# Attention with talking heads and two MLPs: loads of v halved and doubled in number, scatters and weight stores regrouped

## The chip, the cores and the metric

The program runs on one core of one Trainium2 chip. The metric is the time of one execution on the device, in microseconds; the median of 3 runs stands for a kernel. One execution was also taken by the hardware profiler, and all rows below are of that one. The engines are named as the profile names them: PE (TensorE, with its weight loads as PEld), DVE (VectorE), ACT (ScalarE), POOL (GpSimd) and SP (SyncE), whose queue issues nearly all DMAs here.

## What is computed

Four batches, twelve heads, 448 rows, 64 values a head. Scores of all heads are mixed by a 12x12 matrix before the softmax and its result by another one after it; then come the product with v and two MLPs over 1792 tokens of 768 values.

```python
scores = scale * np.matmul(q, k.transpose(0, 1, 3, 2))
scores = np.einsum('bhij,hg->bgij', scores, w_pre)
scores = scores - np.max(scores, axis=-1, keepdims=True)
attn = np.exp(scores)
attn = attn / (np.sum(attn, axis=-1, keepdims=True) + 1e-09)
attn = np.einsum('bhij,hg->bgij', attn, w_post)
out = np.matmul(attn, v)
# x: out as (tokens, heads * values)
x = (1 / (1 + np.exp(-(x @ w_gate))) * (x @ w_val)) @ w_out
h = np.maximum(x @ w_in, 0.0)
y = h * h @ w_out2
```

All is in float32; where PE multiplies in a faster format (fp32r), an operand is split into a rounded part and its remainder (gh and gl, wh and wl, xh and xl) and three products are summed.

## The kernel before

**Tiles and groups.** A batch's 448 rows are cut into four tiles of 110, 110, 110 and 118 rows; sixteen tiles in all. For a tile, `scores` (L162) multiplies q and k for six pairs of heads; the result of each head is copied out of PSUM into a tile `e` (even heads of a pair by ACT, L176, odd ones by DVE, L174), and a DMA scatters it into `g` (L181), where a partition holds one row of one head and ten rows of all twelve heads make a *group* of 120 partitions. A tile has 11 groups, the fourth one 12, the last of only 8 rows; 180 groups in all. There are three `e` buffers, of two heads each.

**The loop.** `attention` writes its instructions in an order laid out by hand, one step s a group: `premix` (L206) of group s, `maximum` (L214) on DVE, `exponent` (L222) on ACT, `normal` (L228 to L233) on DVE and POOL, `split` of group s + 2 (cast gh on ACT, L196; remainder gl on POOL, L197), then, as a small planner of costs in microseconds allows (`STEP`, `PW`, `VW`, `SW`), the six `scores` of the next tile, `postmix` (L248) of earlier groups and `values` (L277). Two tiles are a *chunk*; when the postmix of a chunk's last group is done, six value steps of two heads each follow, one a step, and each result is stored to `xs` (L293). Chunks 0, 2, 4 and 6 are the first halves of the batches; their value steps fall where the scores of the batch's fourth tile are computed and scattered.

**Loads of v.** `v_load` (L267) brings `HV` = 4 heads in one DMA of 448 KB into one of two buffers; a chunk needs three. The two first of the program are loaded at s = 4 and 6, each further one after the value step that frees a buffer.

**Scatter of the fourth tile.** 118 rows in order r, r + 10, r + 20, ...: 8 places of a group have 12 rows and 2 have 11, so a head goes out as two DMAs, 8x12 rows and 2x11 rows. The other tiles take one, 10x11.

**Queues.** Every engine, and SP's queue with it, works in the order written. A DMA that must wait for its source, for a free buffer or for the eighth DMA before it holds up all that stand behind it on the same queue.

**The MLP beside it.** `mlp` is a generator, advanced by `whole` while attention still runs: attention yields 1 (every third step from step 68 on), 2 (each step once the last scores are done) or 3 (in the tail), and `EACH` says how many steps of the MLP a yield of each kind may take. These steps load x tiles of finished batches (L559), split them (cast xh on ACT L575, remainder xl on POOL or DVE L576) and prepare the first weights. A weight passes seven stages: load (`w_load`, L451), `w_bias` (ACT), `w_high` and `w_low` (DVE), `w_sum` (POOL, L501; the sum is also stored to `ws`, L502, for the second half of the tokens), `w_round` (ACT, L508) and `w_rest` (POOL, L514). In the MLP's own stage a `tick` before each product advances the even stages and the odd ones in turn.

Of the kernel before, what the change touches and what calls it, by code (L numbers as in the profile page):

```python
# [7 lines left out]
F32 = mybir.dt.float32  # L8
# [8 lines left out]
P = 128  # L17
JP = 112
GI = 10
HV = 4  # L20
LAG = 3
LA = 5
NA = 9
# [1 line left out]
KB = 10  # L25
EARLY = 112
EM = 2
EACH = (1, 2, 2)


def row_tiles(S):
# [3 lines left out]
    return list(zip(cuts, cuts[1:]))  # L35


def row_order(i0, i1):

    return [i for r in range(GI) for i in range(i0 + r, i1, GI)]  # L40


def attention(tc, q, k, v, w_pre, w_post, xs, B, H, S, D):
# [10 lines left out]
    nc = tc.nc  # L54
    JT = S // JP
# [19 lines left out]
    with ExitStack() as ctx, ExitStack() as mid, ExitStack() as left:  # L75
        kw = dict(side="right")
        one = ctx.enter_context(tc.tile_pool(name="a_one", bufs=1, **kw))
        pv = ctx.enter_context(tc.tile_pool(name="a_v", bufs=2, **kw))
        po = ctx.enter_context(tc.tile_pool(name="a_o", bufs=4, **kw))
        pp = ctx.enter_context(tc.tile_pool(name="a_p", bufs=1, **kw))  # L80
        pa = mid.enter_context(tc.tile_pool(name="a_a", bufs=NA, **kw))
# [32 lines left out]
        def mixers():  # L114
            wp32 = p0.tile([KM, GI, H], F32, name="wp32")
            nc.vector.tensor_tensor(
                out=wp32, in0=mask, in1=wr[:, 0:1, :].to_broadcast([KM, GI, H]), op=ALU.mult
            )
            nc.vector.tensor_scalar(out=wp32, in0=wp32, scalar1=SCALE, scalar2=None, op0=ALU.mult)
            x = wp32.rearrange("p i g -> p (i g)")  # L120
            nc.vector.tensor_copy(wp[0], x)
            nc.vector.tensor_tensor(out=wp[1], in0=x, in1=wp[0].bitcast(F32), op=ALU.subtract)
            nc.vector.tensor_tensor(
                out=wq.rearrange("p g i -> p i g"),
                in0=mask,
                in1=wr[:, 1:2, :].to_broadcast([KM, GI, H]),
                op=ALU.mult,
            )
# [14 lines left out]
            nc.sync.dma_start(out=q_t[n][:, p0:p1, :isz], in_=x[:, p0:p1])  # L143


        g_t = {}

        def scores(n, p):

            b, i0, isz = tiles[n]  # L150
            if p == 0:
                g_t[n] = pg.tile([KM, GT, S], F32, tag="g", name="g")
            kt = k_t.pop((b, p)) if i0 + isz == S else k_t[b, p]
            ps = [
                ps_b.tile([P, S], F32, tag="b", name="ps_s")
                if n == 0 and p % 2
                else ps_q.tile([P, S], F32, tag="q", name="ps_s")
                for _ in range(2)
            ]
            for o in range(2):  # L160
                r = slice(o * D, (o + 1) * D)
                nc.tensor.matmul(  # L162
                    ps[o][:isz], lhsT=q_t[n][r, p, :isz], rhs=kt[r], start=True, stop=True
                )
            if n == 0 and p >= 3:
                e = [pa.tile([IM, S], F32, tag="a", name="e0") for _ in range(2)]
            else:
                t = p4.tile([IM, 2, S], F32, tag="e", name="e")
                e = [t[:, o] for o in range(2)]
            ng, rest = divmod(isz, GI)  # L170
            to = g_t[n].rearrange("(r h) g j -> h r g j", h=H)
            for o in range(2):
                if o:
                    nc.vector.tensor_copy(e[o][:isz], ps[o][:isz])  # L174
                else:
                    nc.scalar.copy(e[o][:isz], ps[o][:isz])  # L176
                queue = nc.scalar if n == 0 and o and p in (1, 3, 4, 5) else nc.sync
                for r0, r1, g in ((0, rest, ng + 1), (rest, GI, ng)):
                    if r0 < r1:
                        e0 = r0 * (ng + 1)  # L180
                        queue.dma_start(  # L181
                            out=to[2 * p + o, r0:r1, :g], in_=e[o][e0 : e0 + (r1 - r0) * g]
                        )


        a_t = {}
# [76 lines left out]
        vraw = {}  # L263

        def v_load(c, hv):
            t = pv.tile([JP, HV, JT, D], F32, tag="vraw", name="vraw")
            nc.sync.dma_start(out=t, in_=v[chunks[c][0], hv])  # L267
            vraw[c, hv] = t

# [69 lines left out]
        for p in range(NP):  # L339
            scores(0, p)  # L340
        mixers()
        q_load(1)
        for s in range(2):
            split(s)
        for s in range(NG + 30):
            if s < NG:
                premix(s)
            flush()
            if s < NG:
                maximum(s)  # L350
            if s in (4, 6):
                load_next(v_load, v_order)
            if 8 <= s < 8 + KB - NP:
                load_next(k_load, k_order)
            if 1 <= s <= NG:
                exponent(s - 1)
            if 2 <= s < NG + 2:
                normal(s - 2)
            if s + 2 < NG:
                split(s + 2)  # L360
            left_over = STEP - MW
            ready = front and front[0][0] <= s
            if ready and due(s):
                next_scores()
                ready, left_over = False, left_over - SW
            fresh = None
            while bpos < len(back) and (left_over > 0.5 or s >= NG):
                f, cost, *x = back[bpos]
                if f is postmix:
                    if x[0] > s - LAG:  # L370
                        break
                    fresh = groups[x[0]][3]
                elif x[0] == fresh:
                    if s < NG:
                        break
                    flush()
                if len(pending) > 3:
                    flush()
                f(*x)
                if f is values and (x[1] + 2) % HV == 0:  # L380
                    pending.append((load_next, v_load, v_order))
                bpos += 1
                left_over -= cost
                if f is postmix and x[0] == NG - 1:
                    flush()
                    mid.close()
                if s >= NG:
                    yield 3 if bpos == len(back) or back[bpos][0] is values else 2
            if ready and left_over > 0.4:
                next_scores()  # L390
            if not front and not closed:
                left.close()
                closed = True
            if NG - EARLY <= s < NG:
                if closed:
                    yield 2
                elif s % 3 == 0:
                    yield 1
# [3 lines left out]
def mlp(tc, xs, wg, wv, wo, wi2, wo2, out, DM, DF1, DF2):  # L402
# [6 lines left out]
    nc = tc.nc  # L409
# [5 lines left out]
    with ExitStack() as ctx:  # L415
# [83 lines left out]
        def w_sum(n):  # L499
            s, x = size(n), w32[n]  # L500
            nc.gpsimd.tensor_tensor(out=x[:, s], in0=x[:, s], in1=fs.pop(n)[:, s], op=ALU.add)  # L501
            nc.sync.dma_start(out=ws[n, :, s], in_=x[:, s])  # L502

        def w_round(n):
            s = size(n)
            h = pw.tile([P, KC, P], F32R, tag="wh", name="wh")
            lo = pw.tile([P, KC, P], F32R, tag="wl", name="wl")
            nc.scalar.copy(h[:, s], w32[n][:, s])  # L508
            ready[n] = (h, lo)

        def w_rest(n):
            s = size(n)
# [288 lines left out]
```

## Time and profile before

| | |
|---|---|
| median of 3 runs | 1525.56 us (1524.79 to 1530.44) |
| the profiled execution | 1525.78 us, span 1524.1 us |
| busy: PE, DVE, ACT, POOL | 1473.3, 804.6, 580.3, 709.0 us |
| PE busy in the first 50 us | 33.3 us |
| PE busy from 50 to 500 us | 420.6 of 450 us |
| PE busy from 550 us to the end | 970.5 of 974 us |

A row of a timeline gives the start in us from the program's start, the duration, the engine and line, what is written and read, how many instructions are merged, and in brackets how long the engine was idle before it and what ended that. SPq and ACTq are the queues of SP and ACT: the row is the issue of a DMA, not its transfer. Matmuls are pipelined and their ends modelled, so rows of PE overlap a little. A wait is put down to the semaphore that came last by the profile; at a cast that waits for many scatters at once the name shown can be that of another DMA.

### The profile page before, as it was taken

Reading aid. Unit: us, or ns where it says so; the run is one execution under the profiler, and the core shown is the slowest. Engines: PE = TensorE matmul, PEld = TensorE weight load, DVE = VectorE, ACT = ScalarE, POOL = GpSimd, SP = SyncE. Lnnn points to the kernel's source line nnn. Section 1 sums busy time; section 2 is a strip of 40 time slices with the busy share of each in tenths; the row PEclk is TensorE's granted clock in tenths of the full one; section 3 lists DMA queues with packets and bytes.
Section 4 is the critical chain, followed back from the end, with each engine's and each line's share of the span. In section 5 each row is a group of like instructions: output and inputs, shape, how many; then the busy total and the mean of one; then the engine's idle time right before and its main releaser. Section 6 shows DMA issues by size and latency. Waiting matters only on the chain.

```text
span 1524.1 us, 21978 instructions
## 1 busy us (share of the span) xinstructions
PE 1473.3 (97%) x8028; PEld 1248.1 (82%) x8028; DVE 804.6 (53%) x1367; ACT 580.3 (38%) x1192; POOL 709.0 (47%) x583
## 2 busy tenths in 40 slices
PE   6989979999997999999999999999999999999999
PEld 2666747667676889999999999999999999999998
DVE  3747748667675576768889998921111101333000
ACT  3645645655654333332334443312222111333111
POOL 3756647657766455454545555532222222223221
PEclk8999989999998999999999999999999999999999
DMA  5554554555534254444444456632112111112221
GB/s 168 151 156 127 144 157 119 160 166 149 159 117 122 80 168 159 174 156 165 156 157 163 165 163 197 218 111 63 52 52 63 52 46 59 52 52 62 77 71 41
DMA packets 84400, 185.47 MB, mean 122 GB/s; under 512 B 17348, under 2 KB 54212, under 8 KB 84292
## 3 DMA queue, kind: packets, MB, share of 16 engines
q1 hardware_dynamic: 83812, 183.28, 38.3%
q8 instruction: 63, 1.03, 0.3%
q10 hardware_dynamic: 480, 0.79, 0.1%
q14 instruction: 45, 0.37, 0.1%
HBM read 107.75 MB, written 37.75 MB: 95 GB/s over the span
## 4 chain that ended last, share of the span: by engine, by line
PE 90%; DMA 5%; POOL 1%; issue 1%; DVE 1%; SPq 1%; ACT 1%; ACTq 0%; POOLq 0%
PE ps L643 66%; PE ps_p L248 8%; PE ps_m L206 6%; PE ps_s L162 5%; PE ps_v L277 4%; DMA xr<-xs 1%; DMA vraw<-in_v 1%; DMA q<-in_q 1%; DMA g<-e 1%; POOL gl L197 1%; DMA k<-in_k 1%; SPq L181 1%; POOL wn L233 1%; DVE xl L576 0%; DVE e L174 0%
## 5 line engine op out<-in xcount | busy, mean ns | idle before, releaser
L514 POOL TENSOR_TENSOR wl<-w,wh 128x768 fp32r<-128x768 f32 (+1 forms) x140 | 258.6, 1849 | 553.9 <-ACT wh L508 546.0
L643 PE MATMUL ps<-xh,wh 128*128 128x448 f32 x960 | 352.2, 367 | 0.0
L643 PE MATMUL ps<-xh,wl 128*128 128x448 f32 x960 | 351.7, 366 | 0.0
L643 PE MATMUL ps<-xl,wh 128*128 128x448 f32 x960 | 351.7, 366 | 0.0
L643 PE MATMUL ps<-hh,wl 128*128 128x448 f32 x672 | 247.0, 368 | 0.0
L643 PE MATMUL ps<-hl,wh 128*128 128x448 f32 x672 | 247.0, 368 | 0.0
L643 PE MATMUL ps<-hh,wh 128*128 128x448 f32 x672 | 246.9, 367 | 0.0
L197 POOL TENSOR_TENSOR gl<-g,gh 120x448 fp32r<-120x448 f32 x180 | 208.0, 1156 | 23.5 <-ACT gh L196 23.5
L248 PEld LDWEIGHTS ps_p<-wn,a 120*112 120x112 f32 (+1 forms) x1440 | 164.2, 178 | 39.3 <-issue 18.7
L643 PEld LDWEIGHTS ps<-xh,wh 128*128 128x128 f32 x960 | 180.4, 188 | 16.5 <-issue 1.0
L643 PEld LDWEIGHTS ps<-xh,wl 128*128 128x128 f32 x960 | 180.4, 188 | 15.4 <-POOL wl L514 0.2
L643 PEld LDWEIGHTS ps<-xl,wh 128*128 128x128 f32 x960 | 180.5, 188 | 14.9
L248 PE MATMUL ps_p<-wn,a 120*112 120x120 f32 (+1 forms) x1440 | 176.5, 271 | 2.7 <-POOL wn L233 2.7
L233 POOL TENSOR_SCALAR wn<-wq,sm 120x120 f32<-120x120 f32 x180 | 107.1, 595 | 153.2 <-DVE sm L231 114.0
L214 DVE TENSOR_REDUCE nm<-ps_m 120x1 f32<-120x448 f32 x180 | 111.9, 622 | 96.6 <-PE ps_m L206 96.4
L501 POOL TENSOR_TENSOR w<-w,w_f 128x768 f32<-128x768 f32 (+1 forms) x70 | 135.4, 1934 | 58.5 <-DVE w_f L490 58.5
L206 PE MATMUL ps_m<-gh,wp 120*120 120x448 f32 x360 | 121.4, 419 | 18.0 <-ACT gh L196 10.7
L661 DVE TENSOR_TENSOR ps<-ps,sg 128x448 f32<-128x448 f32 x48 | 30.4, 632 | 201.8 <-PE ps L643 201.8
L643 PEld LDWEIGHTS ps<-hh,wh 128*128 128x128 f32 x672 | 126.3, 188 | 11.5
L643 PEld LDWEIGHTS ps<-hl,wh 128*128 128x128 f32 x672 | 126.3, 188 | 11.5
L643 PEld LDWEIGHTS ps<-hh,wl 128*128 128x128 f32 x672 | 126.2, 188 | 11.5
L222 ACT ACTIVATE a<-ps_m,nm 120x448 f32<-120x448 f32 x180 | 114.7, 637 | 42.3 <-DVE nm L214 41.4
(45 smaller groups left out, 1690.2 us busy)
## 6 DMA issues: line engine op xcount, KB each, us to landing
g<-e SPq DMA_DIRECT2D x140, 192.5 KB
ws<-w SPq DMA_DIRECT2D x58, 384.0 KB
w<-ws SPq DMA_DIRECT2D x58, 384.0 KB
w_raw<-in_wo SPq DMA_DIRECT2D x18, 768.0 KB
w_raw<-in_wi SPq DMA_DIRECT2D x16, 768.0 KB
vraw<-in_v SPq DMA_DIRECT2D x24, 448.0 KB
w_raw<-in_wg SPq DMA_DIRECT2D x12, 768.0 KB
w_raw<-in_wv SPq DMA_DIRECT2D x12, 768.0 KB
```

Of the source, the lines that this page charges most:

```text
L162: nc.tensor.matmul(ps[o][:isz], lhsT=q_t[n][r, p, :isz], rhs=kt[r], start=True, stop=True)
L197: nc.gpsimd.tensor_tensor(out=lo[:kk], in0=x, in1=hi[:kk].bitcast(F32), op=ALU.subtract)
L206: nc.tensor.matmul(ps[:kk], lhsT=wp[w][:kk, :kk], rhs=x, start=m == 0, stop=m == 2)
L214: nc.vector.tensor_reduce(out=nm[:kk], in_=ps[:kk], op=ALU.max, axis=AX.X, negate=True)
L222: nc.scalar.activation(a[:kk], ps[:kk], AF.Exp, bias=nm[:kk], accum_out=sm[:kk])
L233: nc.gpsimd.tensor_scalar(out=wn[:kk], in0=wq[:kk], scalar1=sm[:kk], scalar2=None, op0=ALU.mult)
L248: nc.tensor.matmul(ps[:JP, jt], lhsT=a[:kk, jt * JP : (jt + 1) * JP], rhs=wn[:kk].rearrange("p g i -> p (g i)"), start=True, stop=True,)
L277: nc.tensor.matmul(ps[o * D : (o + 1) * D, :w], lhsT=vraw[c, (h + o) // HV][:, (h + o) % HV, jt, :], rhs=ap[c][:, jt, h + o, :w], start=jt ...
L501: nc.gpsimd.tensor_tensor(out=x[:, s], in0=x[:, s], in1=fs.pop(n)[:, s], op=ALU.add)
L514: nc.gpsimd.tensor_tensor(out=lo[:, s], in0=w32.pop(n)[:, s], in1=h[:, s].bitcast(F32), op=ALU.subtract)
L643: nc.tensor.matmul(ps, lhsT=a, rhs=x, start=first and n == 0, stop=last and n == total - 1)
L661: nc.vector.tensor_tensor(out=pv, in0=pv, in1=sg[c], op=ALU.mult)
```

## The change

- `HV` is 2: v comes in six loads a chunk instead of three, 224 KB each, into four buffers (as many bytes as before). The first four are issued at s = 4, 5, 6 and 7; each further one after every value step.
- Rows of a tile are ordered by whole groups: the fourth tile's head goes out as one DMA of 10x11 rows and one of its last 8 rows.
- The first tile of the program is scattered in two passes: groups 0 to 3 at once (40 rows a head), groups 4 to 10 (70 rows) after all six pairs and the mixers, and before the q load of the second tile.
- A yield of kind 2 takes one step of the MLP instead of two.
- The store of a prepared weight moves from `w_sum` to `w_round`.

```diff
-HV = 4
+HV = 2
-EACH = (1, 2, 2)
+EACH = (1, 1, 2)
...
-def row_order(i0, i1):
-
-    return [i for r in range(GI) for i in range(i0 + r, i1, GI)]
+def blocks(b, i0, i1):
+
+    n = (i1 - i0) // GI
+    return [(0, 4), (4, n)] if b == i0 == 0 else [(0, n)]
+
+
+def row_order(b, i0, i1):
+
+    rows = []
+    for g0, g1 in blocks(b, i0, i1):
+        rows += [i0 + g * GI + r for r in range(GI) for g in range(g0, g1)]
+    return rows + list(range(i0 + len(rows), i1))
...
-        pv = ctx.enter_context(tc.tile_pool(name="a_v", bufs=2, **kw))
+        pv4 = ctx.enter_context(tc.tile_pool(name="a_v", bufs=4, **kw))
...
-                queue = nc.scalar if n == 0 and o and p in (1, 3, 4, 5) else nc.sync
-                for r0, r1, g in ((0, rest, ng + 1), (rest, GI, ng)):
-                    if r0 < r1:
-                        e0 = r0 * (ng + 1)
-                        queue.dma_start(
-                            out=to[2 * p + o, r0:r1, :g], in_=e[o][e0 : e0 + (r1 - r0) * g]
-                        )
+                e0 = 0
+                for m, (g0, g1) in enumerate(blocks(b, i0, i0 + isz)):
+                    e1 = e0 + (g1 - g0) * GI
+                    move = (to[2 * p + o, :, g0:g1], e[o][e0:e1])
+                    if m:
+                        second.append(move)
+                    else:
+                        queue = nc.scalar if n == 0 and o and p in (1, 3, 4, 5) else nc.sync
+                        queue.dma_start(out=move[0], in_=move[1])
+                    e0 = e1
+                if e0 < isz:
+                    nc.sync.dma_start(out=to[2 * p + o, : isz - e0, g1], in_=e[o][e0:isz])
...
         mixers()
+        for x, y in second:
+            nc.sync.dma_start(out=x, in_=y)
         q_load(1)
...
-            if s in (4, 6):
+            if s in (4, 5, 6, 7):
                 load_next(v_load, v_order)
...
             nc.gpsimd.tensor_tensor(out=x[:, s], in0=x[:, s], in1=fs.pop(n)[:, s], op=ALU.add)
-            nc.sync.dma_start(out=ws[n, :, s], in_=x[:, s])
...
             ready[n] = (h, lo)
+            if n < once:
+                nc.sync.dma_start(out=ws[n, :, s], in_=w32[n][:, s])
```

The order on PE is the same in both kernels. On SP's queue, at the program's start, before (g is the group tile, e a score copy, wr the two mixing matrices):

```order
L101 DMA wr<-in_w_post 120x1x12
L181 DMA g<-e 10x11x448 x5
L181 DMA g<-e_183 10x11x448
L181 DMA g<-e_193 10x11x448
L181 DMA g<-e_203 10x11x448
L143 DMA q<-in_q 128x6x110
L181 DMA g<-e 10x11x448 x8
```

and now:

```order
L110 DMA wr<-in_w_post 120x1x12
L193 DMA g<-e 10x4x448 x5
L193 DMA g<-e_183 10x4x448
L193 DMA g<-e_193 10x4x448
L193 DMA g<-e_203 10x4x448
L356 DMA g<-e 10x7x448 x6
L356 DMA g<-e_183 10x7x448
L356 DMA g<-e_184 10x7x448
L356 DMA g<-e_193 10x7x448
L356 DMA g<-e_194 10x7x448
L356 DMA g<-e_203 10x7x448
L356 DMA g<-e_204 10x7x448
L152 DMA q<-in_q 128x6x110
```

The q load of the second tile has moved behind twelve more scatters. SP's queue at chunk 0's value steps, from the fifth pair of heads of the fourth tile on, before:

```order
L181 DMA g<-e 8x12x448
L181 DMA g<-e 2x11x448
L135 DMA k<-in_k 128x448
L293 DMA xs_57<-xo 128x220 x2
L267 DMA vraw<-in_v 112x1024
L181 DMA g<-e 8x12x448
L181 DMA g<-e 2x11x448
L181 DMA g<-e 8x12x448
L181 DMA g<-e 2x11x448
```

and now:

```order
L193 DMA g<-e 10x11x448
L196 DMA g<-e 8x448
L144 DMA k<-in_k 128x448
L306 DMA xs_57<-xo 128x220
L280 DMA vraw<-in_v 112x512
L306 DMA xs_57<-xo 128x220
L280 DMA vraw<-in_v 112x512
L193 DMA g<-e 10x11x448
L196 DMA g<-e 8x448
L193 DMA g<-e 10x11x448
L196 DMA g<-e 8x448
```

A half load of v now stands behind each store of a value step, the first of them one store sooner. On ACT at chunk 6's value steps, from the third value copy xo on, before:

```order
L292 COPY xo<-ps_v 128x220
L222 ACTIVATE a,sm<-ps_m,nm 120x448
L196 CAST gh<-g 120x448
L575 CAST xh<-xr 128x448
L508 CAST wh<-w_3880 128x768
L292 COPY xo<-ps_v 128x220
L222 ACTIVATE a,sm<-ps_m,nm 120x448
L196 CAST gh<-g 120x448
L575 CAST xh<-xr 128x448
```

and now, from the fourth on:

```order
L305 COPY xo<-ps_v 128x220
L235 ACTIVATE a,sm<-ps_m,nm 120x448
L209 CAST gh<-g 120x448
L591 CAST xh<-xr 128x448
L522 CAST wh<-w_3920 128x768
L305 COPY xo<-ps_v 128x220
L235 ACTIVATE a,sm<-ps_m,nm 120x448
L209 CAST gh<-g 120x448
L305 COPY xo<-ps_v 128x220
L235 ACTIVATE a,sm<-ps_m,nm 120x448
L209 CAST gh<-g 120x448
L591 CAST xh<-xr 128x448
```

The first cast of an x tile stands a group later, the second two groups behind it instead of one.

## Rows read from the trace of the kernel before

**Rows 1.** Page: busy us (share of the span) x instructions of each engine
```profile
PE 1473.3 (97%) x8028; PEld 1248.1 (82%) x8028; DVE 804.6 (53%) x1367; ACT 580.3 (38%) x1192; POOL 709.0 (47%) x583
```

**Rows 2.** windows: stretch, length, busy PE PEld DVE ACT POOL, PEclk, DMA share, GB/s
```profile
0.00:50.00 50.00, 33.33 (x155) 18.07 (x156) 22.52 (x55) 21.10 (x48) 19.72 (x29) 0.86 0.61 173
50.00:500.00 450.00, 420.63 (x2824) 297.22 (x2823) 299.83 (x764) 252.68 (x640) 298.84 (x341) 0.97 0.49 141
...
550.00:1524.00 974.00, 970.52 (x4752) 892.50 (x4750) 456.05 (x506) 290.94 (x476) 368.82 (x198) 1.00 0.33 111
```

**Rows 3.** waits of PE: who for whom, us in total, times, longest
```profile
PE ps_v L277 <- DMA vraw<-in_v: 13.4, 4, 8.1
```

**Rows 4.** timeline, program's start: start us, us, engine line op, [idle before <-releaser]
```profile
7.15 9.96 SPq L181 DMA_DIRECT2D g<-e  x8
...
9.49 0.79 ACTq L181 DMA_DIRECT2D g<-e  x1
...
12.45 0.53 ACT L176 COPY e<-ps_s 110x448 f32<-110x448 f32 x1 [1.59 <-DVE e L174]
...
17.16 0.64 SPq L143 DMA_DIRECT2D q<-in_q  x1
21.80 1.50 ACT L196 CAST gh<-g 120x448 fp32r<-120x448 f32 x3 [8.82 <-DMA q<-in_q]
...
24.29 1.83 PE L162 MATMUL ps_s<-k,q 64*110 64x448 f32 x4
```

**Rows 5.** windows of 10 us: in the first tile's scatter, and in later ones
```profile
10.00:20.00 10.00, 1.68 (x6) 0.53 (x6) 2.45 (x7) 1.37 (x3) 0.00 (x0) 0.68 0.70 222
...
50.00:60.00 10.00, 10.00 (x61) 6.62 (x60) 7.57 (x21) 6.24 (x17) 6.59 (x8) 1.00 0.64 203
```

**Rows 6.** timelines of PE, ACT, SP at chunk 0's values (78 to 112 us)
```profile
84.63 2.54 PE L277 MATMUL ps_v<-ap,vraw 112*64 112x220 f32 x16 [2.21 <-issue]
...
99.16 3.20 PE L277 MATMUL ps_v<-ap,vraw 112*64 112x220 f32 x16 [2.23 <-DMA vraw<-in_v]
...
83.33 0.53 ACT L176 COPY e<-ps_s 118x448 f32<-118x448 f32 x1 [2.62 <-DMA g<-e]
...
92.89 0.37 SPq L267 DMA_DIRECT2D vraw<-in_v  x1
```

**Rows 7.** timelines of SP, PE at chunk 2's values (195 to 232 us)
```profile
205.34 3.29 SPq L181 DMA_DIRECT2D g<-e  x4
...
216.31 0.33 SPq L267 DMA_DIRECT2D vraw<-in_v  x1
...
206.80 1.71 PE L277 MATMUL ps_v<-ap,vraw 112*64 112x220 f32 x16
...
223.23 3.20 PE L277 MATMUL ps_v<-ap,vraw 112*64 112x220 f32 x16 [8.12 <-DMA vraw<-in_v]
```

**Rows 8.** timeline of PE at chunk 4's values
```profile
344.74 1.71 PE L277 MATMUL ps_v<-ap,vraw 112*64 112x220 f32 x16 [0.85 <-DMA vraw<-in_v]
```

**Rows 9.** timelines of SP, ACT, PE at chunk 6's values (456 to 486 us)
```profile
459.74 1.23 SPq L559 DMA_DIRECT2D xr<-xs  x2
...
466.51 0.56 ACT L575 CAST xh<-xr 128x448 fp32r<-128x448 f32 x1 [8.09 <-DMA xr<-xs]
...
462.39 1.71 PE L277 MATMUL ps_v<-ap,vraw 112*64 112x220 f32 x16 [2.21 <-DMA vraw<-in_v]
468.72 1.10 PE L206 MATMUL ps_m<-gh,wp 120*120 120x448 f32 x2 [4.62 <-ACT a L222]
...
470.13 3.20 PE L277 MATMUL ps_v<-ap,vraw 112*64 112x220 f32 x16
...
483.44 0.67 PE L206 MATMUL ps_m<-gh,wp 120*120 120x448 f32 x2 [2.61 <-ACT a L222]
```

**Rows 10.** windows, columns as in rows 2: the last groups of attention
```profile
490.00:500.00 10.00, 9.78 (x72) 8.09 (x71) 8.91 (x24) 6.00 (x16) 8.92 (x11) 1.00 0.00 1
```

**Rows 11.** waits of SP's queue: who for whom, us in total, times, longest
```profile
SPq L502 <- POOL w L501: 213.8, 67, 32.2
```

More of the change, by code (lines that the diff above doesn't have):

```diff
@@ L143, in q_load @@
             nc.sync.dma_start(out=q_t[n][:, p0:p1, :isz], in_=x[:, p0:p1])
-        g_t = {}
+        g_t, second = {}, []
         def scores(n, p):
@@ L169, in scores @@
                 e = [t[:, o] for o in range(2)]
-            ng, rest = divmod(isz, GI)
             to = g_t[n].rearrange("(r h) g j -> h r g j", h=H)
@@ L265, in v_load @@
         def v_load(c, hv):
-            t = pv.tile([JP, HV, JT, D], F32, tag="vraw", name="vraw")
+            t = pv4.tile([JP, HV, JT, D], F32, tag="vraw", name="vraw")
             nc.sync.dma_start(out=t, in_=v[chunks[c][0], hv])
@@ L775 @@
         "q": np.concatenate(
-            [qt[b][:, :, row_order(i0, i1)].ravel() for b in range(B) for i0, i1 in row_tiles(S)]
+            [qt[b][:, :, row_order(b, i0, i1)].ravel() for b in range(B) for i0, i1 in row_tiles(S)]
         ),
```

## The prediction

> **What bounds the kernel now.** I read the page's engine line first, then the busy time by stretch, then who PE waits for, then the timelines at each wait. PE is busy for 1473.3 of 1524.1 us [rows 1], so all that can be won is PE's idle time and the time after it in which PE runs at its lower clock. From 550 us on PE is busy 970.5 of 974.0 us [rows 2]: nothing is to be had there, only to be lost. Before 550 us PE is idle for 16.7 us of the first 50 and 29.4 us of the next 450 [rows 2]. The 29.4 us are not spread evenly. Most lie at the value matmuls of chunks 0, 2 and 6, which are also where the fourth tile of a batch (118 rows) is scattered. Four waits for loads of v alone make 13.4 us, one of them 8.1 [rows 3].
>
> At each such place the queue of SP is late, and PE finds out through another engine. At chunk 0, ACT waits 2.62 us for a scatter to give back a score buffer [rows 6], and PE then 2.21 us; later PE waits 2.23 us for v. At chunk 2 the v load is issued at 216.31, long after the matmuls that free its buffer (they start at 206.80), and PE stands still for 8.12 us until 223.23 [rows 7]: 6.9 us from issue to use. At chunk 6 ACT, which works in order, stands 8.09 us at the cast of an x tile whose load left SP only at 459.74; PE waits 4.62 and 2.61 us behind ACT, and 2.21 us for v [rows 9]. The granted clock, 0.97 over these 450 us [rows 2], stands behind each long wait at the lower of its two levels, 1.2 GHz of 2.4: sixteen value matmuls take 3.20 us instead of 1.71, two premix matmuls 1.10 instead of 0.67 [rows 7, 9].
>
> **The change part by part.** PE's order of work is the same in both kernels; what moves is SP's queue and, for the x tiles, ACT, DVE and POOL.
>
> *What the three middle waits cost.* Chunk 0: 2.21 + 2.23 idle, and slow matmuls 2.54 - 1.71 and 3.20 - 1.71 [rows 6, 7], 6.8 us. Chunk 2: 8.12 + 1.49, 9.6 us. Chunk 4: 0.85 [rows 8]. Chunk 6: 2.21 + 4.62 + 2.61 + 1.49 [rows 9], 10.9 us. The premix and postmix groups behind these waits run slow too: some five pairs of premix matmuls at 0.43 us more [rows 9] and about 1 us beside them, 3 us. Together 31 us. This is the most that the edits can give back.
>
> *Partial groups apart.* Before, a head of the 118-row tile goes out as 8x12 rows and 2x11 rows; now as 10x11 rows and 8 single rows. SP issues as many DMAs as before, and four of them cost it 3.29 us [rows 7]. A whole one of ten cost 0.79 us on ACT's queue [rows 4]; the single rows lie between 0.33 us, like a v load [rows 7], and 0.82, a quarter of 3.29; so a pair of heads costs SP 2.2 to 3.3 us, and I take 2.9, no real gain in issue. What should improve is the landing. Where only 10x11 scatters run, PE is busy 10.00 of 10 us with DMA at 0.64 [rows 5]; the form now used for nearly all of the tile is the one that holds nobody up. So the 2.62 us wait of ACT should go, and loads queued behind should land in some 4.6 us (the q load of 17.16, used at 21.80 [rows 4]) rather than 6.9.
>
> The Trainium skill ("DMA: Bandwidth & Descriptors", section "Why a DMA increments its semaphore by 16 and not by 1") says that a DMA uses the largest number of engines up to 16 that divides the slowest dimension of both sides, and the lowest-numbered ones. By that rule the 2x11 piece sits on two engines that also carry 12 rows of the other: 23 rows a head there, against 12 after. The trace agrees as far as it shows it: DMA share is 0.70 while ten-row scatters fill the queue [rows 5], near 10 of 16. Were it untrue, both forms would take equally long and the 2.6 us at chunk 0 would stay.
>
> *Values by two heads.* Before, heads 8 to 11 come in one load that must wait for heads 0 to 3; now heads 8 and 9 are loaded once heads 0 and 1 are done. At chunk 2 this puts the load ahead of the next pair's scatter: SP ends the scatter of 205.34 at 208.6, then an x load and a store, so v leaves at about 209.7 and lands at 214.3, against a need at 223.23 - 8.12 = 215.1: no wait. The second half leaves behind one more pair of heads, at about 214.5, and lands at 219.1; heads 10 and 11 follow 8 and 9 by 1.71 us and a premix group of some 0.7, so it is needed at 217.5 and comes 1.6 us late. I keep 1 us at chunk 0 and 1.6 at chunk 2. The 24 more issues cost SP 0.33 us each [rows 7], 8 us over 500; they lie beside PE's work, save in the value steps, where they are in the counts above.
>
> *One feed step instead of two, stores a step later.* In the last groups, x loads and splits come one a group rather than two. The first x cast stands one group later on ACT; its load still follows the last scatter at once, at 459.74. With 4.6 us to land it is there near 464.4. PE ran out of work at 462.39 - 2.21 = 460.2 because of v; without that wait ACT's next group ends, and the cast stands, near 462.5. I keep 1 us of the 4.62, and none of the 2.61, since a later x tile now has about twice the time. The price: two x splits and one weight remainder move on POOL into groups where POOL is already busy 8.91 (DVE) and 8.92 (POOL) of 10 us beside PE's 9.78 [rows 10]: 0 to 4 us (all hidden, or all added), I take 1. The stores of weights keep their place in SP's queue relative to the loads from the eleventh load on, so in the long stage nothing moves; SP waits up to 32.2 us at one [rows 11], yet PE is full in that stage [rows 2]. I cost them at 0 (-1 to +1). Gain so far 31 - 3.6 - 1, about 26 us.
>
> *First tile in two passes.* The first group needs only rows 0 to 39, so its cast starts earlier than 21.80 [rows 4]. But the q load of the second tile, issued at 17.16 behind eight scatters, now stands behind twelve more, and PE's second piece of work, the scores at 24.29, needs it. The last score copy is done at 12.45 + 0.53 = 12.98; two issues of 0.79 and a gap later, near 14.8, the first pass is out. Twelve issues at 0.79 plus gaps of 0.07 end at 25.1; 4.6 us on, PE gets q at 29.7: 5.4 us later than 24.29. One more step at the low clock adds 1. Bounds: at 0.33 us an issue, as for a v load, nothing is lost; at 1.25 (9.96 for eight [rows 4]) from 17.1, with 6.9 us to land, 15 us. I take 6.4, by the nearest row, the single 0.79: no backlog remains when each DMA carries 70 rows. What follows shifts with it, as PE has little idle time to give back outside the places named.
>
> **Sum.** -26 + 6.4 is -19.6 us. The profiled execution took 1525.78 us (span 1524.1), the median of the runs is 1525.56; the same difference gives 1506, and I say 1505, as some 1 us of slow clock beside the waits is not in the terms.
>
> **The rivals.**
> (a) SP stays the limit. Its pairs still cost 2.9 to 3.3 us plus k, store and v, and the queue is late again at chunks 0 and 2, and x loads leave no sooner. For it: four issues back to back already take 3.29 us [rows 7]. Against: v now passes one pair of heads. Half of the 31 us comes back: -15.5 + 6.4, 1516.
> (b) Half loads land no sooner than whole ones. Loads keep their 6.9 us [rows 7]; then 3 us stay at chunk 0, 4 at chunk 2, 3 at chunk 6: -20 + 6.4, 1512. The Trainium skill (the same page, section "Anatomy of one DMA — SWDGE (gpsimd) path") fits about 2 us of fixed time beside the bytes; by that a half load saves little in landing. The rows show no half load; the gain that I count is in the earlier release.
> (c) Slower: the q load behind the second pass. If each issue waits as the eight did (1.25 us) and q lands late, PE restarts near 39 us: +15. It decides from where the later places give back under 7 us, as when (a) holds fully and v and x stay late. Then 1525.6 + 15 - 5, 1536.
> (d) The edits do all that they can and the second pass is issued cheaply: -31 + 3, 1498.
>
> **How the numbers follow.** Forecast 0.62 (1499 to 1511), (a) 0.13, (b) 0.12, (c) 0.05, (d) 0.08. The range 1495 to 1517 takes in the forecast, (b), (d) and most of (a). A measurement of this kernel can tell about 0.5% (7.6 us) from no change: faster, below 1518, takes the forecast, (b), (d) and a third of (a), 0.86; same, the rest of (a) and a little of (c), 0.10; slower 0.04.
>
> **What would show it.** At the start, the first cast of g near 17 us, and a PE wait for q of some 10 us behind the first premix, where the kernel before has none. No long wait of ACT for a scatter near 83; v waits below 2 us at chunks 0, 2 and 6 in place of 13.4; no wait of 8 us for x. PE's busy time after 550 us (later or sooner by the shift) is as before. The forecast is wrong if SP issues v in chunk 2 more than 6 us after its release, or if a PE wait for weights appears behind the moved stores.

## The result: 1506.3 us, 1.3% faster, and the profile after

The changed kernel takes 1506.3 us (median of 4 runs, 1505.05 to 1507.58) where the kernel before takes 1525.7 (4 runs); the ratio is 0.9867, with an interval of 0.9845 to 0.9889. That is faster by more than the 0.5% a measurement can tell. The profiled execution took 1505.82 us (span 1503.7), 20.4 us of span less than before.

The page of the kernel after, its busy times (as rows 1) and the chain by engine:

```profile
PE 1463.7 (97%) x8028; PEld 1244.1 (83%) x8028; DVE 805.1 (54%) x1367; ACT 580.2 (39%) x1192; POOL 710.6 (47%) x583
...
PE 95%; DMA 2%; issue 1%; POOL 1%; SPq 1%; DVE 0%; ACT 0%; ACTq 0%; POOLq 0%
```

Windows, columns as in rows 2 (stretch, length, busy time of PE, PEld, DVE, ACT and POOL, granted clock, DMA share, GB/s):

```profile
0.00:50.00 50.00, 31.03 (x134) 17.12 (x134) 20.32 (x49) 19.05 (x43) 17.31 (x25) 0.83 0.56 159
50.00:500.00 450.00, 432.48 (x2943) 308.59 (x2944) 309.79 (x791) 261.60 (x659) 311.26 (x355) 0.99 0.50 145
500.00:550.00 50.00, 50.00 (x292) 42.87 (x289) 31.99 (x38) 16.13 (x28) 22.18 (x12) 1.00 0.45 143
```

In the first 50 us PE does 2.3 us less than before, from 50 to 500 us 11.9 us more, at a granted clock of 0.99 instead of 0.97. Whom PE waits for (us in total, times, longest):

```profile
PE ps_s L171 <- DMA q<-in_q: 9.2, 2, 8.2
...
PE ps_p L261 <- POOL wn L246: 5.0, 7, 1.5
...
PE ps_m L219 <- ACT a L235: 3.3, 1, 3.3
...
PE ps_v L290 <- DMA vraw<-in_v: 2.7, 2, 1.8
```

and two of the same waits in the kernel before:

```profile
PE ps_p L248 <- POOL wn L233: 2.7, 6, 0.6
PE ps_s L162 <- DMA q<-in_q: 1.4, 1, 1.4
```

The waits for v are down from 13.4 us [rows 3] to 2.7. The long wait for q is new (9.2 us in all, 1.4 before), and PE waits longer for POOL's small product wn (5.0 us, 2.7 before).

**The start** (timelines of PE and SP; the first row is of the kernel before, the others of the kernel after):

```profile
22.41 1.10 PE L206 MATMUL ps_m<-gh,wp 120*120 120x448 f32 x2 [10.74 <-ACT gh L196]
...
18.24 1.10 PE L219 MATMUL ps_m<-gh,wp 120*120 120x448 f32 x2 [5.70 <-ACT gh L209]
...
28.35 1.83 PE L171 MATMUL ps_s<-k,q 64*110 64x448 f32 x4 [8.15 <-DMA q<-in_q]
...
7.16 7.76 SPq L193 DMA_DIRECT2D g<-e  x8
14.97 9.75 SPq L356 DMA_DIRECT2D g<-e  x12
24.76 0.63 SPq L152 DMA_DIRECT2D q<-in_q  x1
```

The first premix starts 4 us sooner than before, but the next scores stand at 28.35 instead of 24.29 [rows 4]: q leaves SP behind twelve scatters, and PE is idle for 8.15 us.

**Chunks 0 and 2** (SP and PE; the first pair of scatter rows stands for all):

```profile
95.97 0.38 SPq L280 DMA_DIRECT2D vraw<-in_v  x1
...
97.46 0.80 SPq L193 DMA_DIRECT2D g<-e  x1
98.31 0.69 SPq L196 DMA_DIRECT2D g<-e  x1
...
99.69 1.71 PE L290 MATMUL ps_v<-ap,vraw 112*64 112x220 f32 x16 [0.88 <-DMA vraw<-in_v]
...
209.58 0.38 SPq L280 DMA_DIRECT2D vraw<-in_v  x1
...
214.22 0.38 SPq L280 DMA_DIRECT2D vraw<-in_v  x1
...
218.25 2.89 PE L290 MATMUL ps_v<-ap,vraw 112*64 112x220 f32 x16 [1.80 <-DMA vraw<-in_v]
```

Where PE stood still for 8.12 us at chunk 2 [rows 7], it now waits 1.80, for the load of heads 10 and 11, which is issued 4.03 us before its use instead of 6.9; the value matmuls behind that wait still run slow (2.89 us). ACT's wait for a scatter near 83 us [rows 6] is gone.

**Chunk 6** (SP, ACT, PE):

```profile
451.40 0.44 SPq L575 DMA_DIRECT2D xr<-xs  x1
...
454.52 0.56 ACT L591 CAST xh<-xr 128x448 fp32r<-128x448 f32 x1 [4.49 <-DMA xr<-xs]
...
456.74 0.66 PE L219 MATMUL ps_m<-gh,wp 120*120 120x448 f32 x2 [3.31 <-ACT a L235]
...
457.44 3.29 PE L261 MATMUL ps_p<-wn,a 120*112 120x120 f32 x16
...
478.56 1.07 PE L261 MATMUL ps_p<-wn,a 120*112 120x120 f32 x8 [1.45 <-POOL wn L246]
```

ACT's 8.09 us at the x tile [rows 9] have become 4.49; PE still loses 3.31 behind it, and the postmix after it runs at the lower clock (3.29 us, where 1.80 is usual). The waits for POOL lie in the groups behind.

**A table for all kernels.** (The kernels other than before and after are those of the experiments below.) PE's order of work hardly differs between them, so places can be compared by the start of a chunk's first value matmuls in the timelines of PE. The stretches from chunk 1 to 2, 3 to 4 and 5 to 6 are 55.6, 57.7 and 55.6 us in all, within 0.1 (one exception, 58.4); what differs is in these columns (us; one profiled execution each):

| kernel | to chunk 0 | 0 to 1 | 2 to 3 | 4 to 5 | 6 to 7 | 7 to the end |
|---|---|---|---|---|---|---|
| before | 84.6 | 63.2 | 69.5 | 62.3 | 68.6 | 1007.0 |
| before, second profile | 86.0 | 62.7 | 68.7 | 62.3 | 68.3 | 1007.0 |
| before + scatter | 87.1 | 62.9 | 66.2 | 63.4 | 67.6 | 1006.9 |
| before + v | 89.1 | 60.0 | 66.9 | 61.3 | 67.8 | 1004.1 |
| before + scatter + v | 85.3 | 58.8 | 60.3 | 62.5 | 66.0 | 1004.1 |
| before + one feed step | 87.6 | 63.3 | 69.3 | 62.8 | 63.9 | 1004.1 |
| before + stores | 89.0 | 64.2 | 68.2 | 63.3 | 70.6 | 1006.9 |
| after, two feed steps | 88.8 | 58.7 | 64.3 | 61.4 | 68.8 | 1004.1 |
| after, one pass | 84.5 | 58.5 | 60.4 | 61.3 | 60.8 | 1004.1 |
| after, q first | 81.9 | 58.7 | 62.4 | 61.4 | 61.8 | 1004.1 |
| after | 88.1 | 58.7 | 62.2 | 59.8 | 62.0 | 1004.1 |
| experiment 9 | 81.2 | 58.6 | 60.5 | 62.7 | 63.8 | 1004.2 |
| experiment 10 | 82.2 | 58.1 | 60.5 | 62.7 | 63.0 | 1004.1 |
| experiment 11 | 83.0 | 58.1 | 60.3 | 59.8 | 67.5 | 1004.1 |

After against before: +3.5 at the start, -4.5, -7.3, -2.5 and -6.6 at chunks 0, 2, 4 and 6, and -2.9 behind the last chunk, where nothing was expected. The first column differs by up to 4.5 us between profiles of kernels with the same start (84.6 to 89.1), so a single figure in it says little.

### The profile page after: what moved, and what is told of

Its sections match the earlier page's. It is cut to its first block, busy times and chain, and to the rows that moved or that the text cites. A ratio compares the mean times of both kernels' runs of the same rounds, so it can differ in the third digit from the quotient of the medians.

```text
span 1503.7 us, 22073 instructions
## 1 busy us (share of the span) xinstructions
PE 1463.7 (97%) x8028; PEld 1244.1 (83%) x8028; DVE 805.1 (54%) x1367; ACT 580.2 (39%) x1192; POOL 710.6 (47%) x583
## 4 chain that ended last, share of the span: by engine, by line
PE 95%; DMA 2%; issue 1%; POOL 1%; SPq 1%; DVE 0%; ACT 0%; ACTq 0%; POOLq 0%
PE ps L659 66%; PE ps_p L261 10%; PE ps_m L219 8%; PE ps_s L171 6%; PE ps_v L290 5%; DMA q<-in_q 1%; DMA vraw<-in_v 0%; POOL wn L246 0%; POOL gl L210 0%; SPq L356 0%; DMA k<-in_k 0%; DMA xr<-xs 0%; DMA g<-e 0%; POOL xl L592 0%; SPq L193 0%
## 5 line engine op out<-in xcount | busy, mean ns | idle before, releaser
L273 DVE COPY ap<-ps_p 112x480 f32<-112x480 f32 x180 | 116.8, 652 | 22.1 <-PE ps_p L261 22.0
```

The costliest lines, as they stand in the source:

```text
L273: nc.vector.tensor_copy(ap[c][:, :, :, g0 - i0 : g0 - i0 + rows], ps[:JP, :, :, :rows])
```

## Experiments

The theory: SP's queue and the landing of what it issues make PE wait at chunks 0, 2 and 6; the edits shorten both there, and the second pass costs a part back. Rivals: one edit alone carries the gain; SP's rate of issue stays the limit; the second pass costs nothing in the end. Each kernel is the one before or after with the edit shown. Times are medians, ratios are to the kernel before, timed on the same chip (1525.9, 1526.5 and 1526.6 us in the three groups of runs). A ratio goes by all runs and can differ by some us from that of the medians.

**1. After, q first.**

```diff
         mixers()
+        q_load(1)
         for x, y in second:
             nc.sync.dma_start(out=x, in_=y)
-        q_load(1)
```

> The kernel after with one move: the q load of the second tile is issued before the twelve scatters of the second pass, not behind them. Theory (the q load stands behind these issues on SP, and PE waits for nothing else there): q is issued near 15.0 us in place of 24.76, the PE wait of 8.15 us for q goes, PE does the scores of the second tile near 20.3 in place of 28.35, and of the 8 us some 1.5 come back as a wait for the fifth group, whose rows are in the second pass: 1500 us (1498.5 to 1501.5), 6 us below the kernel after. Rival (the second pass itself is the limit): PE gets its scores early but then stands still for the fifth group's cast, 4 us or more, and the time is 1503 to 1506.

Measured: 1501.06 us (1499.99 to 1501.56), ratio 0.9831 [0.9817, 0.9844]. Timelines of PE and SP:

```profile
17.51 1.10 PE L219 MATMUL ps_m<-gh,wp 120*120 120x448 f32 x2 [5.43 <-ACT gh L209]
...
19.40 1.83 PE L171 MATMUL ps_s<-k,q 64*110 64x448 f32 x4
...
28.22 1.00 PE L171 MATMUL ps_s<-k,q 64*110 64x448 f32 x2 [1.10 <-ACT e L184]
...
14.48 0.63 SPq L152 DMA_DIRECT2D q<-in_q  x1
15.17 9.77 SPq L357 DMA_DIRECT2D g<-e  x12
```

The long wait for q is gone and the second scores stand 9 us sooner; 1.10 us come back at 28.22, behind ACT, whose cast of g at 27.17 waits 2.40 us for a scatter. Chunk 0 is 6.2 us sooner than in the kernel after, and the median is 5.2 us lower. So the q load's place behind the pass was the price, not the pass.

**2. After, one pass.**

```diff
-    return [(0, 4), (4, n)] if b == i0 == 0 else [(0, n)]
+    return [(0, n)]
```

> The kernel after with the first tile scattered in one pass, as before the change. Theory (the second pass costs what the start shows, and nothing gives it back later): the scores of the second tile stand near 24.3 us again in place of 28.35, the work behind them 5.4 us sooner, and the time is 1501 us (1499.5 to 1502.5). Rival (the delay of the start is absorbed by later waits): 1505 to 1507, with longer waits at the chunk steps than in the kernel after.

Measured: 1501.63 us (0.9851 [0.9824, 0.9878]). Five of the six runs lie between 1500.34 and 1502.61, below every run of the kernel after; one took 1513.78, and it widens the interval until it overlaps with that of the kernel after. By the medians, the second pass, as the change has it, costs 4.7 us, and nothing behind it gives that back. Issued behind the q load, as in experiment 1, the pass is worth nothing clear either way (1501.06 against 1501.63).

**3. Before + scatter.** The kernel before with the ordering and the scatter code of the kernel after, and `blocks` as in experiment 2.

```diff
-                for r0, r1, g in ((0, rest, ng + 1), (rest, GI, ng)):
...
+                if e0 < isz:
+                    nc.sync.dma_start(out=to[2 * p + o, : isz - e0, g1], in_=e[o][e0:isz])
```

> The kernel before with only the partial groups scattered apart (10x11 rows and 8 single rows in place of 8x12 and 2x11). Theory (the form changes how fast the scatter lands, not how fast SP issues it): a pair of heads still costs SP about 3 us, ACT's wait of 2.62 us for a scatter near 83 goes, loads of v and x land in about 4.6 us rather than 6.9, so the 8.12 us wait at chunk 2 falls to 5 to 6, and the time is 1517 to 1519 us. Rival (landing is not changed by the form, or does not matter): 1523 to 1526, the waits for v as before.

Measured: 1522.99 us (0.9973 [0.9963, 0.9983]): the time is that of the rival, less gain than expected, while the waits moved as the theory has it. Chunk 2, SP and PE:

```profile
216.96 0.38 SPq L280 DMA_DIRECT2D vraw<-in_v  x1
...
222.31 3.20 PE L290 MATMUL ps_v<-ap,vraw 112*64 112x220 f32 x16 [5.02 <-DMA vraw<-in_v]
```

The load is used 5.35 us after its issue instead of 6.9, and PE's wait falls from 8.12 to 5.02, as expected. ACT's wait for a scatter near 83 us is gone. But chunk 0's wait for v rose from 2.23 to 3.57 us: no longer held up by ACT, PE came to it 10.8 us after the chunk's start instead of 12.3, while the load left SP as late as before (8.4 us after it, and 8.3). From issue to use it took 5.9 us there, and 6.3 in the kernel before: 0.4 us less, where chunk 2 shows 1.5.

**4. Before + v.**

```diff
-HV = 4
+HV = 2
...
-            if s in (4, 6):
+            if s in (4, 5, 6, 7):
```

with four buffers. 

> The kernel before with only the values loaded by two heads in four buffers. Theory (the early release is what helps): at chunk 2 the load of heads 8 and 9 leaves SP near 210 in place of 216.31; landing is still 6 to 7 us, so the wait there falls from 8.12 to 2 to 4 us; the waits for v at chunks 0 and 6 (2.23 and 2.21) fall to under 1; ACT's scatter wait at 83 and the x wait at chunk 6 stay: 1513 to 1516 us. Rival (half loads land no sooner and SP is the limit): the wait moves to the next pair of heads at nearly full size, 1520 to 1525.

Measured: 1519.07 us (0.9942 [0.9923, 0.9960]), between the two. Chunk 2, SP and PE, and ACT at chunk 0:

```profile
212.82 0.34 SPq L267 DMA_DIRECT2D vraw<-in_v  x1
...
218.73 2.35 PE L277 MATMUL ps_v<-ap,vraw 112*64 112x220 f32 x16 [2.36 <-DMA vraw<-in_v]
...
218.30 0.38 SPq L267 DMA_DIRECT2D vraw<-in_v  x1
...
224.02 3.20 PE L277 MATMUL ps_v<-ap,vraw 112*64 112x220 f32 x16 [1.54 <-DMA vraw<-in_v]
...
87.72 0.53 ACT L176 COPY e<-ps_s 118x448 f32<-118x448 f32 x1 [3.04 <-DMA g<-e]
```

The first half load takes 5.9 us to its use and the second 5.7, with the old scatter form beside them; ACT's wait for a scatter stays. So half a load does land sooner than a whole one (5.9 against 6.9; with the new form 4.0 against 5.35), and the form of the scatter matters as much.

These are single loads. The semaphore updates in the traces tell when each DMA landed. Loads of v issued within 6 us of a scatter of a fourth tile land, in the median, 6.4 us after their issue in the kernel before (6 loads), 5.3 in experiment 3 (7), 5.8 in experiment 4 (15), 3.8 with both edits in experiment 5 (18) and 4.0 in the kernel after (21). The pieces of 8x12 and of 2x11 rows themselves take 5.4 and 5.7 us to land, the pieces of 10x11 and 8 rows that replace them 3.6 and 3.0.

**5. Before + scatter + v.** Experiments 3 and 4 in one kernel.

> The kernel before with the partial groups scattered apart and the values loaded by two heads, the one feed step and the moved stores left out. Theory (these two together make chunks 0, 2 and 4 what they are after the change, and each needs the other; the feed step works at chunk 6 alone): loads of v land in 4 us from issue to use, chunk 2's wait is under 2 us, the waits for x at chunk 6 of 4.62 and 2.61 us stay, and the time is 1507 us (1505 to 1509.5). Rival (the feed step and the stores carry nothing): 1501 to 1503, the time of the kernel after with the first tile in one pass.

Measured: 1506.62 us (0.9872 [0.9851, 0.9893]), as the theory has it. Alone the two edits give 2.9 and 6.9 us by the medians, 4.1 and 8.9 by the ratios; together they give 19.9 and 19.5 (2.9 us of what v gives, alone or with the scatter, lie behind the last chunk, see below). By the timelines chunk 2 gives 3.3 and 2.7 us alone and 9.2 together, chunk 0 0.3 and 3.1 alone and 4.4 together. So each gives more with the other, by how much is less sure: from the start of chunk 0 to the end the profiles have 3.5 and 10.6 alone and 18.9 together. Each of them alone leaves waits at chunk 2 with slow matmuls after them (3.20 us in both fences above); with both, one wait is left, and the matmuls after it are not slow:

```profile
215.28 1.71 PE L290 MATMUL ps_v<-ap,vraw 112*64 112x220 f32 x16 [1.48 <-DMA vraw<-in_v]
```

**6. Before + one feed step, and 7. after with two feed steps.**

```diff
-EACH = (1, 2, 2)
+EACH = (1, 1, 2)
```

and the reverse. 

> The kernel before with only one feed step in place of two in the second part of the interleaved stretch. Theory: the x load still leaves SP near 459.7, but the cast stands a group later on ACT, so of the waits of 4.62 and 2.61 us behind it 2 to 4 us go, less 1 to 2 us of new waits for POOL: 1522.5 to 1524.5 us. Rival (without the earlier v the feed step has no slack to use): 1525 to 1527.

> The kernel after with the two feed steps back. Theory (the one feed step pays for itself): the wait of PE behind the x cast at chunk 6, 3.3 us in the kernel after, grows to 6 to 8 in sum, PE's waits for POOL's wn fall from 5.0 to 2.7, and the time is 1508.5 us (1507.5 to 1510.5). Rival (what the x cast gains POOL takes back): 1505 to 1507.

Measured: 1519.81 us (0.9958 [0.9944, 0.9972]), a larger gain than theory or rival had, and 1511.15 us (0.9911 [0.9888, 0.9935], runs from 1508.53 to 1516.98), a loss a little over the theory's. PE's waits, first of experiment 6, then of 7:

```profile
PE ps_p L248 <- POOL wn L233: 4.4, 6, 1.4
...
PE ps_m L206 <- ACT a L222: 3.1, 1, 3.1
```

```profile
PE ps_m L219 <- ACT a L235: 9.6, 2, 6.3
...
PE ps_p L261 <- POOL wn L246: 2.7, 6, 0.6
```

By the medians the feed step is worth 4.9 us in the kernel after and 6.7 in the kernel before, 2.9 of which lie behind the last chunk (below). It takes the second x wait away whole and leaves one of 3 us; its price is POOL's waits, 5.0 or 4.4 us instead of 2.7.

**8. Before + stores.**

```diff
-            nc.sync.dma_start(out=ws[n, :, s], in_=x[:, s])
...
+            if n < once:
+                nc.sync.dma_start(out=ws[n, :, s], in_=w32[n][:, s])
```

(out of `w_sum`, into `w_round`). 

> The kernel before with only the weight stores issued in the rounding step, a step later. Theory: in SP's queue they keep their place among the loads, so 1524.5 to 1526.5 us, the waits of PE as before. Rival (a store that waits for its sum holds x loads back in SP's queue near chunk 6): 1521 to 1523, with the x wait of 8.09 us on ACT shorter.

Measured: 1527.32 us, ratio 1.0008 [0.9993, 1.0023]. In the kernel before, the stores alone are worth nothing either way.

**9 to 11. Beyond the change.** All three start from experiment 1. In 9 the product wn of the last 24 groups goes to ACT:

```diff
+            if s >= NG - 24:
+                nc.scalar.activation(wn[:kk], wq[:kk], AF.Copy, scale=sm[:kk])
```

> The kernel after with q issued ahead of the second pass (as in the first run), and in the last 24 groups of attention the small product wn on ACT in place of POOL. Theory (with one feed step a group, POOL is the engine that PE waits for near 470 to 480 us: 5.0 us in all): these waits fall to about 1 us, ACT has room for it at 6 of 10 us busy, and the time is 1497.5 us (1496 to 1499.5) against 1501.1 without it. Rival (ACT works in order, and wn behind the exponent is late too): 1501 to 1504, with PE waits for wn on ACT.

In 10 the x loads of the second batch leave on ACT's queue:

```diff
-            nc.sync.dma_start(out=xr[c, i], in_=xs[hf * NC + c][i * P : (i + 1) * P, :])
+            queue = nc.scalar if hf == 0 and c else nc.sync
+            queue.dma_start(out=xr[c, i], in_=xs[hf * NC + c][i * P : (i + 1) * P, :])
```

> The kernel after with q issued ahead of the second pass, and the x loads of the second batch issued on ACT's queue in place of SP's. Theory (the x tile is late at chunk 6 because its load stands behind the scatters on SP): ACT's wait of 4.5 us for the first x tile falls under 1 us, PE's wait of 3.0 to 3.3 us behind it goes with the slow postmix group after it, and the time is 1497 us (1495.5 to 1498.5) against 1501.1. Rival (the x tile is late in landing, not in issue): 1500 to 1502, the wait as it was.

11 has both. 

> Both of the two moves above in one kernel, with q issued ahead of the second pass. If the two waits are apart, as theory has it, the gains add: 1493.5 us (1492 to 1496). Rival (they fill the same hole, or ACT is full with both): 1496 to 1499.

Measured: 1502.85, 1501.54 and 1505.18 us: none beats the 1501.06 of experiment 1. In 9 the rival came true; in 10 its time did, but not its reason, as the wait for x went; 11 is slower than either expectation. Waits of ACT in experiment 9, of SP (stretch of 430 to 456 us) in experiment 10, and ACT's timeline there:

```profile
ACT wn L247 <- DVE sm L244: 17.7, 18, 2.6
```

```profile
SPq L196 <- DMA xr<-xs: 3.9, 1, 3.9
```

```profile
452.77 0.33 ACTq L576 DMA_DIRECT2D xr<-xs  x1
453.20 0.34 ACT L305 COPY xo<-ps_v 128x220 f32<-128x220 f32 x1 [5.84 <-DMA xs<-xo]
```

In 9 wn on ACT waits for DVE's reciprocal, up to 2.6 us, and everything behind it on ACT waits with it. In 10 ACT's wait for x does go (0.4 us in all), but SP holds a scatter for 3.9 us until the x load that ACT issues has landed: SP is freed of a load and waits for it nevertheless. And ACT pays for the issue. The 5.84 us of idle time that the profile puts down to a store of xs end right behind the issue of ACT's next x load, at 452.77; by the semaphores in the trace that issue waits for a scatter of SP, landed at 451.13, and then for POOL's remainder of an x tile, done at 452.74. ACT, which works in order, stands until then. With both moves, in 11, the stretch from chunk 6 to 7 is the longest of the three (67.5 us), with the same idle time of ACT at 7.0 us and PE's waits for v at 5.8 us, where experiment 1 has 2.8; how the two moves add up to that is not shown.

**12. The kernel before, a second profile.**

> The kernel before once more, for a second profile. In the first one a matmul of the long stage between 545 and 695 us takes 206.7 ns from start to start, 486 in 100 us, where the kernel after, whose PE program differs only ahead of that stage, has 202.7 ns, 495 in 100 us. Theory (which of the two paces holds is a matter of how PE enters the stage in one execution, not of the program): either pace may show, and where it shows the faster one the span behind the last chunk is 2.9 us shorter. Rival (the pace belongs to the program): 486 in 100 us again. If it is 486 again, this one run doesn't exclude the theory.

Measured: 1525.96 us. One window of 100 us of the long stage, for before, before again, experiment 6 and after:

```profile
575.00:675.00 100.00, 100.00 (x486) 90.88 (x485) 70.43 (x84) 35.89 (x54) 50.48 (x27) 1.00 0.45 158
```

```profile
575.00:675.00 100.00, 100.00 (x486) 90.81 (x485) 70.64 (x83) 35.74 (x54) 50.47 (x27) 1.00 0.44 160
```

```profile
580.00:680.00 100.00, 100.00 (x495) 92.67 (x494) 73.60 (x82) 36.68 (x55) 53.03 (x28) 1.00 0.44 161
```

```profile
560.00:660.00 100.00, 100.00 (x495) 92.69 (x494) 74.77 (x83) 36.76 (x56) 52.76 (x28) 1.00 0.47 166
```

The second profile of before shows the slower pace again, so it didn't show the pace to vary between executions. Experiment 6, whose PE program is that of before in every operation, name and shape that the trace records, has the faster one, so it isn't a property of PE's own program either.

Over all fourteen profiles the pace goes by the kernel: slow in the four of kernels that have neither the halved v loads nor the one feed step (before twice, before + scatter, before + stores), fast in the ten that have one of them or both. Either edit alone brings the faster pace (experiments 4 and 6). Why is not shown.

## Why the prediction was right, point by point

The forecast of 1505 us is 1.3 from the result. The mechanism was right: the waits that it named shrank, and the q load was late as it said. That it came so near is in part luck: of its terms some were off, and they offset each other, with the help of 2.9 us that it did not have at all.

- **Partial groups apart: right.** A pair of heads was to cost SP 2.9 us; its four issues take 0.79 to 0.80 and 0.66 to 0.69 us, 2.9 together. Nothing was gained in issue; landing was, 5.35 us from issue to use with this edit alone (experiment 3) and 4.0 with half loads as well, where I took 4.6. That 4.6 was a wrong reading: the cast at 21.80 [rows 4] reads g and waits for scatters, not for q; by the trace's semaphore updates the q load of 17.16 landed at 22.48, 5.3 us after its issue. The rule of the Trainium skill that I weighed ("DMA: Bandwidth & Descriptors", section "Why a DMA increments its semaphore by 16 and not by 1") put the 2x11 piece on two engines that are loaded already; that the scatter wait goes and loads land sooner by the form alone (0.4 us at chunk 0, 1.5 at chunk 2, experiment 3) agrees with it. So do the numbers of semaphore updates in the trace: 16 for a load, 11 for 10x11 rows, 9 for 8x12 and for 8 single rows, 3 for 2x11, that is one a DMA engine by that rule and one more where fewer than 16 take part. Which engines they are no row shows.
- **Values by two heads: right at the places read.** The first half was to be on time at chunk 2 and the second 1.6 us late: no wait, and 1.80. Chunk 0 was to keep 1 us: 0.57 and 0.88. Gain at chunk 0: 3.6 expected without the wait ahead of it, 4.5 measured; at chunk 2: 8.0 and 7.3, less since the matmuls behind the 1.80 took 2.89 us, for which I had no term. Rival (b), that half loads land no sooner, fell: 5.9 against 6.9 us with the old scatters at chunk 2, 5.8 against 6.4 in the medians. The fit that the prediction named beside it (the Trainium skill, "DMA: Bandwidth & Descriptors", section "Anatomy of one DMA — SWDGE (gpsimd) path") is of another path than SP's queue. Here half a load landed 0.6 us sooner than a whole one beside the old scatters and 1.5 beside the new (medians of experiments 3 to 5). Experiments 3 to 5 show what the prediction didn't say: its 31 us needed both edits at once.
- **The feed step: right in sign, a third too large at its place.** Of chunk 6's 10.9 us I kept 1 for x and 1 for POOL, a gain of 8.9; the table shows 6.6. The step that failed is the meeting of load and cast: moved with the shift of the place (10.8 us sooner), I had put ACT at the cast near 451.7 and the load's landing near 453.6; ACT was there at 450.0 and the data at 454.5. The load left SP at 451.40, 2.5 us later than the place's shift would have it, right behind the four scatters of a pair of heads, and landed in 3.1 us instead of 4.6. So PE lost 3.31 us, and 1.5 more in the slow postmix, which had no term. POOL's price was 2.3 us (5.0 less 2.7), inside the 0 to 4 that I gave.
- **Weight stores: right.** 0 expected, 1.0008 [0.9993, 1.0023] measured.
- **First tile in two passes: right in kind, 1.7 us too dear.** 6.4 expected, 4.7 measured by the medians (experiment 2). The first pass ends at 14.92 (14.8 expected), the twelve issues at 24.72 (25.1); but q is used 3.6 us after its issue, not 4.6, so PE restarts at 28.35 and not at 29.7.
- **Chunk 4: 2.5 us instead of 0.85.** All but the kernel after and experiment 11 (59.8 both) show 61.2 us or more there, 1 us below before. In every profile PE stands idle for some 2.6 us ahead of chunk 4's first value matmuls, a wait that the prediction missed; the matmuls behind it ran at the full clock in these two and in the second profile of before (1.71 us), and took 2.46 to 3.20 in the rest, 2.74 in the first profile of before. One kernel shows both, so that part is luck of one execution.
- **Behind 550 us: wrong.** I had nothing there (-1 to +1); 2.9 us came, from the pace of matmuls below, which the halved v loads and the one feed step each bring (experiments 4 and 6), by a way that is not known. Without it the forecast would have been 4 us too low: chunks 0 to 6 gave 20.9 us and the wait ahead of chunk 0 1.6 (2.21 [rows 6] less the 0.57 left), together 22.5 instead of the 26 that I counted.
- **The rivals.** SP as the limit (1516) is refuted at chunks 0 and 2 by v waits of 0.88 and 1.80 us, though at chunk 6 it is still SP that is late. The second pass at +15 us is refuted by experiment 2 (4.7). That the edits do all they can (1498) is nearly what experiment 1 reaches (1501.06 us), but it needs the q load ahead of the pass, or no second pass.

## What to carry to other kernels

Count every DMA that a regrouped pass puts ahead of a load that the critical engine needs: one load moved ahead of twelve scatters is worth as much as the whole second pass costs. Two edits on one queue can each look small and be worth more together than their sum (13.0 and 19.5 us here by the ratios), since each alone leaves a wait, and slow matmuls behind it. Moving a late DMA to another engine's queue doesn't free the old queue if its later DMAs wait for it, and it stops the new engine where the issue has to wait.

## What the runs showed of the hardware

- **Two paces of the same matmuls.** From 25 to 180 us behind the start of chunk 7, PE is busy throughout at a granted clock of 1.00, with the same matmuls by name, shape and order (addresses are not in the trace); yet a 128x448 matmul with its weights takes 206.7 ns from start to start in some kernels and 202.7 in others (486 and 495 in 100 us). The slower pace holds in before (both profiles), before + scatter and before + stores, the faster one in all the rest, that is in every kernel with halved v loads or the one feed step. It makes the 2.9 us of the table's last column. What sets it stays open.
- **The start varies.** Among the kernels whose first pass is the same (before and its variants) chunk 0 begins between 84.6 and 89.1 us, so a term of 2 us there can't be read from one profile; the medians had to decide.
- **The form of a scatter changes how soon it lands, and how soon what stands behind it does.** As 8x12 and 2x11 rows a head's pieces took 5.4 and 5.7 us from issue to landing, as 10x11 and 8 single rows 3.6 and 3.0 (medians of 48 each, kernels before and after); loads of v beside them landed in 5.3 us instead of 6.4 (experiment 3).
- **Single rows are not cheap.** The issue of a DMA of 8 rows costs SP 0.66 to 0.69 us, one of 110 rows 0.77 to 0.80, one of 40 rows 0.97 (7.76 for eight, with what they wait) and one of 70 rows 0.81.
